# A software-pipelined attention and routing stage: a tile's sums move to the head of a step, its transposes a step later, and a group's ranks come from products with ones

## The chip, the cores and the metric

The kernel runs on 1 core of one Trainium2 chip. The metric is device time in microseconds (us) of one launch, lower is better. Engines are named as in the profile: PE is TensorE (PEld its weight loads), DVE is VectorE, ACT is ScalarE, POOL is GpSimd, SP is SyncE, which issues most of the DMAs.

## The reference

Three layers follow each other: a gated linear attention, a mixture of experts with one expert per token, and a gated linear unit with a norm. The change touches the first and the routing into the second.

```python
# attention: B, H, S, D = 4, 8, 768, 48
f = 1.0 / (1.0 + np.exp(-f_logit))
for t in range(S):
    state = f[:, :, t, :, None] * state + np.einsum('bhd,bhe->bhde', k[:, :, t], v[:, :, t])
    y[:, :, t] = np.einsum('bhd,bhde->bhe', q[:, :, t], state)
# experts: N, D, E, F = 3072, 384, 8, 1024
logits = x @ w_gate + modality_bias[modality_id]
e_idx = np.argmax(logits, axis=1)
probs = np.exp(logits - logits.max(-1, keepdims=True))
probs /= probs.sum(-1, keepdims=True) + 1e-09
gate_w = probs[np.arange(N), e_idx]
...
    h = np.maximum(x[mask] @ w1[e], 0.0)
    out[mask] = gate_w[mask, None] * (h @ w2[e])
# gated linear unit: d_ff = 1536
xn = x / rms * rms_g
out = (silu(xn @ w_gate) * (xn @ w_val)) @ w_out
```

## The kernel before

**Tiles.** The 3072 tokens are cut into 24 tiles of 128: tile t is chunk t // 4 of batch t % 4, so that the recurrence over chunks of one batch goes from tile t to tile t + 4. Within a chunk the recurrence is a product: running sums of the log gates (`cum`), their exponentials (`em`, `ep`) multiplied into k and q, a masked product (`am`), and a state per batch.

**Steps.** `attention_fast` is written out by hand: a loop over steps s, in which each engine gets its instructions in program order. A tile goes through these pieces, each in a step of its own:

- `p0(t)`: a clamp of the gate logits on DVE (L105), then exp, ln and a cast on ACT (L107, L108, L113), and the low half `ll` on POOL (L115).
- `p1(t)`: the running sums `cum` on PE (L124, L125, into the PSUM tile `pm`), their clamp `bc` on DVE (L129), `em` and `ep` on ACT (L133), `kp` on DVE (L134), `qp` on POOL (L135), and two small DMAs on SP that bring the chunk's decay to `dd` (L138).
- `p2(t)`: eight transposes on PE (L152), copied out by DVE (`kt`) and ACT (`qt`) (L154).
- `p3(t)`: `pa` on PE (L163), the mask product `am` on DVE (L166).
- `p4(t)`: the output `py` on PE (L178, L180), its copy `xt` on ACT (L182), the minimum of the decays `gm` on DVE (L185), the state's update on PE (`pu`, L190), DVE (L197, L199) and POOL (L201). The last chunk (tiles 20 to 23) has no update, the first (0 to 3) no product with the state.
- `mix(t)`: the gate's parts of the logits on PE (L423, into another part of the PSUM tile `pu`), copied by ACT (`ql`, L425); `logits(t)`: their sum on PE (L435, into another part of `pm`).
- Tiles are routed in groups of 4, 4, 2, 3, 3, 2, 2, 1, 1, 1 and 1. At a group's last tile `logits` adds the bias on DVE (`lg`, L438), `route` picks the expert in five DVE operations (L447 to L459) and an exp on ACT (L462), `share` makes the gate's weight (L471 to L474), `ranks` counts on PE (L483, L484, into `pm`) and copies the result (L486), and `place` turns counts into row numbers on DVE (L497 to L511).
- `send(1)`: four transposes `px` on PE (L523), a scaled copy `xo` on ACT (L526), and a scatter by POOL to the expert's rows in DRAM (L527). In the steps of `TWICE` two tiles are sent.

In a step of before, PE gets p4 of tile s-4, logits of s-5, ranks of s-6, p3 of s-3, p2 of s-2, mix of s-4, `cum` of s-1, and px. ACT gets xt, qt, ql, em, ep, the gates' exp, ln and cast of tile s+1, and xo.

**What rides along.** `first(s, x)` runs, at slots 0 to 3 of a step, pieces of the first expert's work that `early` has put on a list: the choice of the expert (`regs`), loads and splits of its weights (`load`, `halves`: L787, L789), gathers (L766), transposes of the gathered rows (`turn`: L805, L715, L716) and, in the last steps, its products (`up`, `down`: L828, L842). After the loop the remaining experts and the gated unit follow, with PE as the busiest engine.

**Order.** Tiles of a pool wait for their buffers' last readers; each engine waits at the head of its own queue. Of PSUM, `pm`, `pu`, `pk`, `pq` and `py` have one bank each and `pa` two.

Of the kernel before, what the change touches and what calls it, by code (L numbers as in the profile page):

```python
# [7 lines left out]
F32 = mybir.dt.float32  # L8
# [3 lines left out]
AF = mybir.ActivationFunctionType  # L12
# [24 lines left out]

TWICE = (15, 16, 23, 26)
LCLAMP = 40.0
# [23 lines left out]
def attention_fast(tc, io, cst, ps, gate, plan, first):  # L63
    nc = tc.nc
    q, k, v, f = io
    ident, tri, mask4, onesc = cst["ident"], cst["tri"], cst["mask4"], cst["onesc"]
    gm = cst["gm"]
    with ExitStack() as ctx:
        ld = ctx.enter_context(tc.tile_pool(name="a_ld", bufs=4))
        wk = ctx.enter_context(tc.tile_pool(name="a_wk", bufs=2))  # L70
        st = ctx.enter_context(tc.tile_pool(name="a_st", bufs=1))
        NB = 3
        qp = [st.tile([P, H, 64], F32, name=f"qp{i}") for i in range(2)]
        kp = [st.tile([P, H, 64], F32, name=f"kp{i}") for i in range(NB)]
        dd = [st.tile([P, HP], F32, name=f"dd{i}") for i in range(6)]
        sb = st.tile([P, B, HP, 2 * D], F32, name="state")
# [3 lines left out]
        def blank():  # L80
            for x in (kp[1], qp[1], kp[2]):
                nc.gpsimd.memset(x[:, :, D:64], 0.0)
            for i in range(6):
                nc.gpsimd.memset(dd[i], 1.0)
            nc.vector.memset(ps["y"], 0.0)
# [16 lines left out]

        def p0(t):
            d = T[t]
            nc.vector.tensor_scalar_max(d["f"], d["f"], -LCLAMP)  # L105
            e = wk.tile([P, H * D], F32, tag="e", name="e")
            nc.scalar.activation(e, d["f"].rearrange("p h d -> p (h d)"), AF.Exp, scale=-1.0)  # L107
            nc.scalar.activation(e, e, AF.Ln, bias=onesc)  # L108
            if t == 0:
                d["l"] = e  # L110
                return
            lh = wk.tile([P, H * D], F32R, tag="lh", name="lh")
            nc.scalar.copy(lh, e)  # L113
# [4 lines left out]
        def p1(t):  # L118
            d = T[t]
            cum = pm[:, 0:DM]  # L120
# [11 lines left out]
            for x, sign in both if t else both[::-1]:  # L132
                nc.scalar.activation(x, b4, AF.Exp, scale=sign)  # L133
            nc.vector.tensor_tensor(out=kp[t % NB][:, :, 0:D], in0=d["k"], in1=em, op=ALU.mult)  # L134
# [34 lines left out]
        def p4(t):  # L169
# [33 lines left out]
        with tc.manual_schedule():  # L203
            for t, names in ((0, "fq"), (1, "f"), (0, "k"), (1, "q"), (1, "k"), (2, "f"), (0, "v"), (1, "v"), (2, "v")):
                load(t, names)
            p0(0)
            setup = gate.setup()
            for s in range(NTILE + 7):
                if s == 1:
                    blank()  # L210
                if s == 3:
                    next(setup)
                    nc.gpsimd.memset(sb, 0.0)
                if s == 7:
# [31 lines left out]
            first(NTILE + 7, 0)  # L246


def decay_flag(tc, top, cst, pt):

    nc = tc.nc
    m1 = top.tile([P, 1], F32, name="fl_m1")
    nc.vector.tensor_reduce(out=m1, in_=cst["gm"], op=ALU.min, axis=AX.X)
    pt = pt()[0:1, 0:P]
# [63 lines left out]
def attention_again(tc, cst, gate, xd):  # L318
    nc = tc.nc
    list(gate.setup())  # L320
    with tc.tile_pool(name="s_x", bufs=9) as xp:
        for t in range(NTILE):
# [7 lines left out]
            gate.logits(t)  # L330
            gate.turns(gate.route(t))
            gate.share(t)
            gate.ranks(t)
# [4 lines left out]
def consts(tc, top, st):  # L338
# [5 lines left out]
    onesc = c["onesc"] = st.tile([P, 1], F32, name="onesc")  # L344
    gm = c["gm"] = top.tile([P, HP], F32, name="gm")
    nc.vector.memset(onesc, 1.0)
# [9 lines left out]
class Gate:  # L356
# [12 lines left out]
    def fill(self, st, w_gate, bias, mod):  # L369
# [39 lines left out]
        nc.vector.tensor_tensor(out=self.tril, in0=cst["tri"].bitcast(F32), in1=cst["ident"], op=ALU.subtract)  # L409
        nc.vector.memset(self.base, 0.0)  # L410
        yield

# [27 lines left out]
    def route(self, t):  # L440
# [18 lines left out]
        nc.vector.tensor_tensor(out=oh, in0=eq, in1=mw.unsqueeze(2).to_broadcast(sh), op=ALU.is_equal)  # L459
        yield  # L460
        self.ex = wk.tile(sh, F32, tag="ex", name="ex")
        nc.scalar.activation(self.ex, sf, AF.Exp)  # L462

    def share(self, t):
# [6 lines left out]
        nc.vector.reduce_sum(sm, self.ex, axis=AX.X)  # L471
        nc.vector.tensor_scalar_add(sm, sm, 1e-9)
        self.gt = wk.tile([P, n], F32, tag="gt", name="gt", bufs=4)
        nc.vector.reciprocal(self.gt, sm)  # L474

    def ranks(self, t):
        if not self.last_of(t):
            return
        n = GROUPS[GOF[t]]
        nc, wk, pm = self.nc, self.wk, self.cst["pm"]  # L480
        self.roh, self.rgt = self.oh, self.gt
        o2 = self.oh.rearrange("p b e -> p (b e)")
        nc.tensor.matmul(pm[:, DM + 32:DM + 32 + n * E], self.tril, o2, start=True, stop=True)  # L483
        nc.tensor.matmul(pm[:, DM + 64:DM + 64 + n * E], self.one16, o2, start=True, stop=True)  # L484
        self.rt = wk.tile([P, 2, n * E], F32, tag="rt", name="rt")
        nc.vector.tensor_copy(self.rt, pm[:, DM + 32:DM + 96].rearrange("p (a x) -> p a x", a=2)[:, :, 0:n * E])  # L486

    def place(self, t):
# [4 lines left out]
        sh = [P, n, E]  # L493
        oh, gt = self.roh, self.rgt
        rt = self.rt.rearrange("p a (b e) -> p a b e", e=E)
        for b in range(n):
            nc.vector.tensor_tensor(out=self.base[:, b + 1, :], in0=self.base[:, b, :], in1=rt[:, 1, b, :], op=ALU.add)  # L497
            yield
# [220 lines left out]
class Experts:  # L719
# [194 lines left out]
    def early(self, plan, ps, pm):  # L914
# [77 lines left out]

        f = FIRST + 7
        on(f, 2, regs)
# [23 lines left out]
        on(n + 7, 0, down, 2)  # L1018
        on(n + 7, 0, halves, 7)
        on(n + 7, 0, up, 5)  # L1020
        on(n + 7, 0, halves, 7)
        on(n + 7, 0, down, 3)
        on(n + 7, 0, up, 6)
        on(n + 7, 0, ahead)
        on(n + 7, 0, down, 4)
        on(n + 7, 0, up, 7)
        for m in (5, 6):
            on(n + 7, 0, down, m)
        on(n + 7, 0, second)
        on(n + 7, 0, down, 7)  # L1030
        on(n + 7, 0, last)
        on(n + 7, 0, next, made)
        self.begun = d
# [342 lines left out]
def attention_experts_glu(  # L1376
# [24 lines left out]
    def layers(again):  # L1401
        flag = None
        with ExitStack() as ctx:
            n = "b" if again else "a"
            top = ctx.enter_context(tc.tile_pool(name="top" + n, bufs=1))
            counts = top.tile([P, B + 1, E], F32, name="counts" + n)
            c2 = ctx.enter_context(ExitStack())
            with ExitStack() as c0:
                plan = Plan(tc, c0, c2.enter_context(tc.tile_pool(name="pt" + n, bufs=1, side="right")), counts[:, 0, :])
                with ExitStack() as c1:  # L1410
# [73 lines left out]
```

## Time before and how to read its profile

| | |
|---|---|
| median of 3 runs | 922.44 us (922.26 to 926.68) |
| profiled execution, its own time | 928.45 us |
| its span, first to last instruction | 926.9 us |
| PE busy in the span | 851.5 us (92%) |
| DVE, ACT, POOL busy | 513.4 (55%), 351.8 (38%), 201.3 us (22%) |
| mean granted clock of TensorE | 0.975 |

The profile is one execution on the chip; its times are us from the span's start. A row of the timeline has the start, the duration, the engine, the source line, the operation, the tile written and the tiles read, and how often; brackets give the idle time of that engine just before, and what ended it. Matmuls are pipelined, so the distance from one group's start to the next tells more than a group's own duration. A table by stretches gives busy us and instruction counts of PE, PEld, DVE, ACT and POOL, then the granted clock (1.00 is 2.4 GHz, 0.50 is 1.2 GHz), the mean busy share of the DMA engines, and GB/s.

### The profile page before, as it was taken

To read this page: it belongs to the slowest core of one execution; us is meant where nothing else is said; L and a number is where in the kernel's file an instruction comes from. 1 tells how busy PE (TensorE), PEld (TensorE's weight loads), DVE (VectorE), ACT (ScalarE), POOL (GpSimd) and SP (SyncE) were. 2 spreads that over 40 slices of the span, in tenths; PEclk is the share of its full clock that TensorE was granted. 3 is DMA by queue.
4 is the path that set the end of the run, shared out by engine and by line. 5 is a ranking of instruction groups with operands and counts; after the bars stand their busy time and mean duration, and the time that the engine had idled before them with its cause. 6 is when DMAs were issued, how large, how long until landed. Compare 5 with 4: busy or idle time off the path is not lost.

```text
span 926.9 us, 13938 instructions
## 1 busy us (share of the span) xinstructions
PE 851.5 (92%) x5218; PEld 717.1 (77%) x5218; DVE 513.4 (55%) x1059; ACT 351.8 (38%) x637; POOL 201.3 (22%) x245
## 2 busy tenths in 40 slices
PE   5789696779999999899899999999999999999993
PEld 4678575667787887678687788888888888888883
DVE  5777687767576665544699937235433622622220
ACT  6656546533444554333433422231231232122121
POOL 4355546422321231112131210010010000001001
PEclk9999998899999999999999999999999999999998
DMA  9776657111653653625222200000000000000001
GB/s 178 140 147 130 132 125 191 61 61 45 200 176 126 194 160 106 124 71 186 69 84 58 64 35 1 0 35 1 1 35 1 1 17 18 1 1 35 1 1 38
DMA packets 145312, 70.66 MB, mean 76 GB/s; under 512 B 113056, under 2 KB 140192, under 8 KB 145232
## 3 DMA queue, kind: packets, MB, share of 16 engines
q1 hardware_dynamic: 140336, 55.18, 24.1%
q0 software_dynamic: 4896, 14.47, 4.6%
q8 instruction: 44, 0.72, 0.3%
q14 instruction: 36, 0.29, 0.1%
HBM read 60.08 MB, written 9.52 MB: 75 GB/s over the span
## 4 chain that ended last, share of the span: by engine, by line
issue 32%; PE 11%; DVE 6%; POOL 2%; DMA 1%; ACT 1%; POOLq 0%; DVEq 0%; ACTq 0%; SPq 0%
PE po L1321 3%; PE pg L1300 3%; PE pv L1300 3%; POOL out_dram L1332 2%; DVE h L1312 1%; DVE q L1151 1%; DVE t L1149 1%; DVE t L1150 1%; PE pr L1235 0%; DVE sg L1309 0%; DVE t L1148 0%; DVE hl L716 0%; DVE h L1311 0%; DMA r<-in_moe_w_val_dram 0%; DMA out_dram<-o,cid 0%
## 5 line engine op out<-in xcount | busy, mean ns | idle before, releaser
L1307 DVE TENSOR_TENSOR h<-sg,pv 128x512 f32<-128x512 f32 x60 | 41.2, 687 | 192.2 <-PE pv L1300 192.2
L1332 POOL DMA_INDIRECT out_dram<-o,cid x24 | 23.2, 965 | 363.5 <-ACT o L1330 361.4
L1306 ACT ACTIVATE sg<-pg 128x512 f32<-128x512 f32 x60 | 35.9, 598 | 147.3 <-PE pg L1300 147.3
L715 ACT CAST hh<-h 128x512 fp32r<-128x512 f32 x70 | 43.3, 620 | 124.1 <-DVE h L1307 113.2
L1300 PE MATMUL pv<-xh,w1h 128*128 128x512 f32 x216 | 85.6, 396 | 2.1 <-DVE xh L1273 2.1
L1300 PE MATMUL pg<-xh,w0h 128*128 128x512 f32 x216 | 86.2, 399 | 0.0
L1300 PE MATMUL pg<-xl,w0h 128*128 128x512 f32 x216 | 85.3, 397 | 0.4 <-DVE xl L716 0.4
L1300 PE MATMUL pv<-xh,w1l 128*128 128x512 f32 x216 | 85.2, 394 | 0.4 <-POOL w1l L1154 0.4
L1300 PE MATMUL pg<-xh,w0l 128*128 128x512 f32 x216 | 85.5, 396 | 0.0
L1300 PE MATMUL pv<-xl,w1h 128*128 128x512 f32 x216 | 85.1, 395 | 0.0
L789 DVE TENSOR_TENSOR l<-r,h 128x768 fp32r<-128x768 f32 x48 | 49.4, 1035 | 33.3 <-ACT h L787 33.0
L716 DVE TENSOR_TENSOR hl<-h,hh 128x512 fp32r<-128x512 f32 x70 | 48.4, 693 | 33.3 <-ACT hh L715 33.3
L1321 PE MATMUL po<-w2h,hh 128*128 128x384 f32 x280 | 62.2, 340 | 2.8 <-ACT hh L715 2.6
L1321 PE MATMUL po<-w2l,hh 128*128 128x384 f32 x280 | 61.7, 338 | 0.0
L1321 PE MATMUL po<-w2h,hl 128*128 128x384 f32 x280 | 61.5, 338 | 0.0
L1321 PEld LDWEIGHTS po<-w2h,hh 128*128 128x128 f32 x280 | 50.7, 188 | 10.1 <-ACT hh L715 4.9
L828 PE MATMUL ph<-xh,h 128*128 128x512 f32 x135 | 54.0, 400 | 0.6 <-ACT xh L715 0.6
L828 PE MATMUL ph<-xh,l 128*128 128x512 f32 x135 | 53.8, 399 | 0.0
L828 PE MATMUL ph<-xl,h 128*128 128x512 f32 x135 | 53.4, 395 | 0.2 <-DVE xl L716 0.2
L787 ACT CAST h<-r 128x768 fp32r<-128x768 f32 x48 | 39.7, 834 | 29.1 <-PE py L842 12.1
L1321 PEld LDWEIGHTS po<-w2l,hh 128*128 128x128 f32 x280 | 50.1, 188 | 0.0
L1321 PEld LDWEIGHTS po<-w2h,hl 128*128 128x128 f32 x280 | 50.1, 188 | 0.0
(316 smaller groups left out, 1822.1 us busy)
## 6 DMA issues: line engine op xcount, KB each, us to landing
r<-in_moe_w_dram SPq DMA_DIRECT2D x48, 384.0 KB, 3.4
f<-in_f_logit_dram SPq DMA_DIRECT2D x24, 192.0 KB, 3.2
q<-in_q_dram SPq DMA_DIRECT2D x24, 192.0 KB, 3.9
k<-in_k_dram SPq DMA_DIRECT2D x24, 192.0 KB, 3.6
v<-in_v_dram SPq DMA_DIRECT2D x24, 192.0 KB, 3.9
r<-in_moe_w_gate_dram SPq DMA_DIRECT2D x12, 384.0 KB, 5.0
r<-in_moe_w_val_dram SPq DMA_DIRECT2D x12, 384.0 KB, 3.5
r<-in_moe_w_out_dram SPq DMA_DIRECT2D x12, 384.0 KB, 3.6
```

The source lines that it names most:

```text
L715: nc.scalar.copy(hi, src)
L716: nc.vector.tensor_tensor(out=lo, in0=src, in1=hi.bitcast(F32), op=ALU.subtract)
L787: self.nc.scalar.copy(h, r)
L789: self.nc.vector.tensor_tensor(out=l, in0=r, in1=h.bitcast(F32), op=ALU.subtract)
L828: nc.tensor.matmul(ph, a[:, kk, c], b[:, kk, 0:T], start=(n == 0), stop=(n == 8))
L1149: V.scalar_tensor_tensor(out=t, in0=top, scalar=-0x40000000, in1=t, op0=ALU.bitwise_and, op1=ALU.bitwise_or)
L1150: V.scalar_tensor_tensor(out=t, in0=low, scalar=29, in1=t, op0=ALU.logical_shift_right, op1=ALU.bitwise_or)
L1300: nc.tensor.matmul(p, a[:, kk, :], b[:, kk, :], start=(n == 0), stop=(n == 8))
L1306: nc.scalar.activation(sg, ps[0], AF.Silu)
L1307: nc.vector.tensor_tensor(out=h, in0=sg, in1=ps[1], op=ALU.mult)
L1321: self.nc.tensor.matmul(po[t], a[:, c], b[:, 0, :], start=(m == 0 and i == 0), stop=(m == self.KF - 1 and i == 2))
L1332: self.apart.add(nc.gpsimd.indirect_dma_start(out=self.out, out_offset=bass.IndirectOffsetOnAxis(ap=self.cid[:, i:i + 1], axis=0), in_=o, ...
```

## The change

From step 4 on, a step begins with p1 of tile s-1 (split into `p1e`, the sums and exponentials, and `p1p`, the products and DMAs), with the clamp of p0 (`p0f`) between them. Then come route of the group that ends at tile s-7, p4 of tile s-4, the exp of that group, the rest of p0 (`p0l`), logits of tile s-6 (before s-5), p3, mix of tile s-5 (before s-4), p2, share and ranks, place, and one send. The loop has 32 steps instead of 31, and the first expert's pieces move by one step with it. The order of the first four steps stays.

The minimum of the decays is not kept tile by tile: `dd` becomes one tile with a place for each of the 24, reduced once at the end. `kp` has four buffers instead of three. The constant 1e-9 is added by a `tensor_tensor` with a tile instead of a `tensor_scalar_add`. The ranks of a group come from n products on the shifted one-hots (its own tile with `tril`, earlier ones with `one16`) and n products for the sums, accumulated in PSUM, now in the bank of `pu`; `place` reads them there, so that the copy `rt`, the n running additions and the copy of the base fall away, and one addition keeps the base.

```diff
-TWICE = (15, 16, 23, 26)
+TWICE = (16, 17, 24, 27)
...
-        NB = 3
+        NB = 4
-        dd = [st.tile([P, HP], F32, name=f"dd{i}") for i in range(6)]
...
         def p0(t):
+            p0f(t)
+            p0l(t)
+        def p0f(t):
+            nc.vector.tensor_scalar_max(T[t]["f"], T[t]["f"], -LCLAMP)
+        def p0l(t):
             d = T[t]
-            nc.vector.tensor_scalar_max(d["f"], d["f"], -LCLAMP)
...
-            x = dd[t % 6]
             for h in range(2):
-                nc.sync.dma_start(x[64 * h:64 * h + D, :], ep[P - 1:P, h])
+                nc.sync.dma_start(dd[64 * h:64 * h + D, t, :], ep[P - 1:P, h])
...
-            x = dd[t % 6]
-            nc.vector.tensor_tensor(out=gm, in0=gm, in1=x, op=ALU.min)
+            x = dd[:, t]
...
-            for s in range(NTILE + 7):
+            for s in range(NTILE + 8):
...
                 first(s, 0)
+
+                full = s >= 4
+                ahead = 0 <= s - 1 < NTILE
+                if full and ahead:
+                    p1e(s - 1)
+                    if s + 1 < NTILE:
+                        p0f(s + 1)
+                    p1p(s - 1)
+                gate.turns(gate.route(s - 7))
                 if 0 <= s - 4 < NTILE:
                     p4(s - 4)
+                gate.exps(s - 7)
+                if full and s + 1 < NTILE:
+                    p0l(s + 1)
                 if s in TWICE:
                     gate.send(1)
-                gate.logits(s - 5)
-                gate.ranks(s - 6)
+                gate.logits(s - 6)
                 first(s, 1)
                 if 0 <= s - 3 < NTILE:
                     p3(s - 3)
+                gate.mix(s - 5)
                 if 0 <= s - 2 < NTILE:
                     p2(s - 2)
                 T.pop(s - 5, None)
-                gate.mix(s - 4)
+                gate.share(s - 7)
+                gate.ranks(s - 7)
                 first(s, 3)
-                gate.turns(gate.route(s - 5))
-                if 0 <= s - 1 < NTILE:
-                    p1(s - 1)
-                gate.turns(gate.place(s - 6))
-                if s + 1 < NTILE:
+                gate.turns(gate.place(s - 7))
+                if not full:
+                    if ahead:
+                        p1(s - 1)
                     p0(s + 1)
-                gate.share(s - 5)
                 gate.send(1)
                 first(s, 2)
...
-        nc.vector.tensor_scalar_add(sm, sm, 1e-9)
+        nc.vector.tensor_tensor(out=sm, in0=sm, in1=self.eps.to_broadcast([P, n]), op=ALU.add)
...
-        nc.tensor.matmul(pm[:, DM + 32:DM + 32 + n * E], self.tril, o2, start=True, stop=True)
-        nc.tensor.matmul(pm[:, DM + 64:DM + 64 + n * E], self.one16, o2, start=True, stop=True)
-        self.rt = wk.tile([P, 2, n * E], F32, tag="rt", name="rt")
-        nc.vector.tensor_copy(self.rt, pm[:, DM + 32:DM + 96].rearrange("p (a x) -> p a x", a=2)[:, :, 0:n * E])
+        rk, sums = pu[:, 192:192 + n * E], pu[:, 224:224 + E]
+        for j in range(n):
+            nc.tensor.matmul(rk[:, j * E:n * E], self.one16 if j else self.tril, o2[:, 0:(n - j) * E], start=(j == 0), stop=(j == n - 1))
+        for b in range(n):
+            nc.tensor.matmul(sums, self.one16, o2[:, b * E:(b + 1) * E], start=(b == 0), stop=(b == n - 1))
...
-        for b in range(n):
-            nc.vector.tensor_tensor(out=self.base[:, b + 1, :], in0=self.base[:, b, :], in1=rt[:, 1, b, :], op=ALU.add)
-            yield
-        nc.vector.tensor_tensor(out=ps_, in0=rt[:, 0], in1=self.base[:, 0:n, :], op=ALU.add)
+        nc.vector.tensor_tensor(out=ps_, in0=rk.rearrange("p (b e) -> p b e", e=E), in1=self.base.unsqueeze(1).to_broadcast(sh), op=ALU.add)
         yield
-        nc.vector.tensor_copy(self.base[:, 0, :], self.base[:, n, :])
+        nc.vector.tensor_tensor(out=self.base, in0=self.base, in1=sums, op=ALU.add)
...
-        f = FIRST + 7
+        f = FIRST + 8
...
-        on(n + 5, 0, up, 3)
-        on(n + 5, 0, down, 1)
-        on(n + 5, 2, next, made)
-        on(n + 7, 0, up, 4)
+        on(n + 6, 0, up, 3)
+        on(n + 6, 0, down, 1)
+        on(n + 6, 2, next, made)
+        on(n + 8, 0, up, 4)
```

## Rows read from the trace of the kernel before

**Rows 1.** Busy time in the stretch of the attention stage.

```profile
20.00:225.00 205.00, 166.90 (x2025) 140.52 (x2022) 148.60 (x421) 113.99 (x222) 95.88 (x126) 0.93 0.52 118
```

**Rows 2.** What PE waited for from 20 to 225 us: total, times, longest.

```profile
PE pu L423 <- ACT xt L182: 11.3, 7, 3.8
PE px L523 <- ACT xo L526: 8.3, 3, 3.9
...
PE pu L423 <- DVE state L197: 2.3, 1, 2.3
```

**Rows 3.** Timeline of the step that ends at 97 us: DVE, ACT, PE.

```profile
93.63 0.35 DVE L105 TENSOR_SCALAR f<-f 128x384 f32<-128x384 f32 x1
...
94.08 0.52 ACT L107 ACTIVATE e<-f 128x384 f32<-128x384 f32 x1 [2.90 <-DVE f L105]
...
96.17 0.58 ACT L182 COPY xt<-py 128x512 f32<-128x512 f32 x1
...
96.80 0.42 PE L423 MATMUL pu<-xt,wg 128*32 128x128 f32 x8 [3.17 <-DVE mx L447]
```

**Rows 4.** Timeline of PE in a step without a stall inside.

```profile
132.94 0.43 PE L423 MATMUL pu<-xt,wg 128*32 128x128 f32 x8 [0.40 <-ACT xt L182]
...
133.76 0.60 PE L523 MATMUL px<-ident,xt 128*128 128x128 f32 x4
134.29 0.43 PE L178 MATMUL py<-qt,state 128*48 128x128 f32 x4
...
138.03 0.66 PE L152 MATMUL pk<-ident,kp 128*128 128x128 f32 x4
138.53 0.60 PE L152 MATMUL pq<-ident,qp 128*128 128x128 f32 x4
```

**Rows 5.** Timeline of DVE over one step with `place` and into the next.

```profile
162.19 0.69 DVE L716 TENSOR_TENSOR xl<-pt,xh 128x512 fp32r<-128x512 f32 x1 [1.83 <-ACT xh L715]
162.79 0.55 DVE L129 TENSOR_SCALAR bc<-pm 128x384 f32<-128x384 f32 x1
163.93 0.56 DVE L134 TENSOR_TENSOR kp<-k,em 128x384 f32<-128x384 f32 x1 [0.59 <-ACT em L133]
164.41 1.59 DVE L497 TENSOR_TENSOR countsa<-countsa,rt 128x8 f32<-128x8 f32 x3
...
167.19 0.95 DVE L789 TENSOR_TENSOR l<-r,h 128x768 fp32r<-128x768 f32 x1
...
168.13 0.71 DVE L199 TENSOR_TENSOR state<-state,pu 48x192 f32<-48x192 f32 x2
...
168.96 1.28 DVE L166 TENSOR_TENSOR am<-pa,mask 128x512 f32<-128x512 f32 x2
...
173.79 0.16 DVE L447 TENSOR_REDUCE mx<-lg 128x2 f32<-128x16 f32 x1
...
174.60 0.17 DVE L459 TENSOR_TENSOR oh<-eq,mw 128x16 bf16<-128x16 f32 x1
```

**Rows 6.** Timeline of POOL at two of its products `qp`.

```profile
154.42 1.20 POOL L135 TENSOR_TENSOR qp<-q,ep 128x384 f32<-128x384 f32 x1 [2.63 <-ACT ep L133]
...
164.78 1.19 POOL L135 TENSOR_TENSOR qp<-q,ep 128x384 f32<-128x384 f32 x1 [3.82 <-ACT ep L133]
```

**Rows 7.** Timeline of DVE: the addition of 1e-9 at two places.

```profile
154.49 1.15 DVE L472 TENSOR_SCALAR sm<-sm 128x3 f32<-128x3 f32 x1
...
195.49 0.17 DVE L472 TENSOR_SCALAR sm<-sm 128x2 f32<-128x2 f32 x1
```

**Rows 8.** Timeline of DVE and PE: the state's update, and the next `mix`.

```profile
125.03 0.72 DVE L199 TENSOR_TENSOR state<-state,pu 48x192 f32<-48x192 f32 x2
...
125.90 0.43 PE L423 MATMUL pu<-xt,wg 128*32 128x128 f32 x8 [1.32 <-DVE state L199]
```

**Rows 9.** Timeline of PE: the second product of `ranks` in one group.

```profile
129.59 0.17 PE L484 MATMUL pm<-oh,one 128*128 128x24 bf16 x1
```

**Rows 10.** Busy time in the stretch behind PE's longest wait of the stage.

```profile
112.60:119.70 7.10, 7.00 (x44) 5.86 (x44) 2.11 (x4) 1.96 (x5) 3.79 (x6) 0.54 0.67 161
```

More of the change, by code (lines that the diff above doesn't have):

```diff
@@ L66, in attention_fast @@
     ident, tri, mask4, onesc = cst["ident"], cst["tri"], cst["mask4"], cst["onesc"]
-    gm = cst["gm"]
+    dd = cst["gm"]
     with ExitStack() as ctx:
@@ L80, in blank @@
         def blank():
-            for x in (kp[1], qp[1], kp[2]):
+            for x in (kp[1], qp[1], kp[2], kp[3]):
                 nc.gpsimd.memset(x[:, :, D:64], 0.0)
-            for i in range(6):
-                nc.gpsimd.memset(dd[i], 1.0)
             nc.vector.memset(ps["y"], 0.0)
@@ L118, in p1, with p1e @@
         def p1(t):
+            p1e(t)
+            p1p(t)
+        def p1e(t):
             d = T[t]
@@ L133, in p1, with p1p @@
                 nc.scalar.activation(x, b4, AF.Exp, scale=sign)
+            d["em"], d["ep"] = em, ep
+        def p1p(t):
+            d = T[t]
+            em, ep = d["em"], d["ep"]
             nc.vector.tensor_tensor(out=kp[t % NB][:, :, 0:D], in0=d["k"], in1=em, op=ALU.mult)
             nc.gpsimd.tensor_tensor(out=qp[t % 2].rearrange("p (a x) d -> p a x d", x=2)[:, :, :, 0:D], in0=d["q"].rearrange("p (a x) d -> p a x d", x=2), in1=ep.rearrange("p x d a -> p a x d"), op=ALU.mult)
-            x = dd[t % 6]
             for h in range(2):
-                nc.sync.dma_start(x[64 * h:64 * h + D, :], ep[P - 1:P, h])
+                nc.sync.dma_start(dd[64 * h:64 * h + D, t, :], ep[P - 1:P, h])
         def p2(t):
@@ L234, in attention_fast @@
                 T.pop(s - 5, None)
-                gate.mix(s - 4)
+                gate.share(s - 7)
+                gate.ranks(s - 7)
                 first(s, 3)
-                gate.turns(gate.route(s - 5))
-                if 0 <= s - 1 < NTILE:
-                    p1(s - 1)
-                gate.turns(gate.place(s - 6))
-                if s + 1 < NTILE:
+                gate.turns(gate.place(s - 7))
+                if not full:
+                    if ahead:
+                        p1(s - 1)
                     p0(s + 1)
-                gate.share(s - 5)
                 gate.send(1)
                 first(s, 2)
-            first(NTILE + 7, 0)
+            first(NTILE + 8, 0)
 def decay_flag(tc, top, cst, pt):
@@ L252, in decay_flag @@
     m1 = top.tile([P, 1], F32, name="fl_m1")
-    nc.vector.tensor_reduce(out=m1, in_=cst["gm"], op=ALU.min, axis=AX.X)
+    nc.vector.tensor_reduce(out=m1, in_=cst["gm"].rearrange("p t a -> p (t a)"), op=ALU.min, axis=AX.X)
     pt = pt()[0:1, 0:P]
@@ L331, in attention_again @@
             gate.turns(gate.route(t))
+            gate.exps(t)
             gate.share(t)
@@ L344, in consts @@
     onesc = c["onesc"] = st.tile([P, 1], F32, name="onesc")
-    gm = c["gm"] = top.tile([P, HP], F32, name="gm")
+    gm = c["gm"] = top.tile([P, NTILE, HP], F32, name="gm")
     nc.vector.memset(onesc, 1.0)
@@ L410, in fill @@
         nc.vector.memset(self.base, 0.0)
+        self.eps = st.tile([P, 1], F32, name="eps")
+        nc.vector.memset(self.eps, 1e-9)
         yield
@@ L459, in route, with exps @@
         nc.vector.tensor_tensor(out=oh, in0=eq, in1=mw.unsqueeze(2).to_broadcast(sh), op=ALU.is_equal)
-        yield
-        self.ex = wk.tile(sh, F32, tag="ex", name="ex")
-        nc.scalar.activation(self.ex, sf, AF.Exp)
+        self.sf = sf
+    def exps(self, t):
+        if not self.last_of(t):
+            return
+        self.ex = self.wk.tile(list(self.sf.shape), F32, tag="ex", name="ex")
+        self.nc.scalar.activation(self.ex, self.sf, AF.Exp)
     def share(self, t):
@@ L479, in ranks @@
         n = GROUPS[GOF[t]]
-        nc, wk, pm = self.nc, self.wk, self.cst["pm"]
-        self.roh, self.rgt = self.oh, self.gt
+        nc, pu = self.nc, self.ps["u"]
+        rk, sums = pu[:, 192:192 + n * E], pu[:, 224:224 + E]
         o2 = self.oh.rearrange("p b e -> p (b e)")
-        nc.tensor.matmul(pm[:, DM + 32:DM + 32 + n * E], self.tril, o2, start=True, stop=True)
-        nc.tensor.matmul(pm[:, DM + 64:DM + 64 + n * E], self.one16, o2, start=True, stop=True)
-        self.rt = wk.tile([P, 2, n * E], F32, tag="rt", name="rt")
-        nc.vector.tensor_copy(self.rt, pm[:, DM + 32:DM + 96].rearrange("p (a x) -> p a x", a=2)[:, :, 0:n * E])
+        for j in range(n):
+            nc.tensor.matmul(rk[:, j * E:n * E], self.one16 if j else self.tril, o2[:, 0:(n - j) * E], start=(j == 0), stop=(j == n - 1))
+        for b in range(n):
+            nc.tensor.matmul(sums, self.one16, o2[:, b * E:(b + 1) * E], start=(b == 0), stop=(b == n - 1))
+        self.rt = rk, sums
     def place(self, t):
@@ L493, in place @@
         sh = [P, n, E]
-        oh, gt = self.roh, self.rgt
-        rt = self.rt.rearrange("p a (b e) -> p a b e", e=E)
-        for b in range(n):
-            nc.vector.tensor_tensor(out=self.base[:, b + 1, :], in0=self.base[:, b, :], in1=rt[:, 1, b, :], op=ALU.add)
-            yield
+        oh, gt = self.oh, self.gt
+        rk, sums = self.rt
         ps_ = wk.tile(sh, F32, tag="ps", name="ps_")
-        nc.vector.tensor_tensor(out=ps_, in0=rt[:, 0], in1=self.base[:, 0:n, :], op=ALU.add)
+        nc.vector.tensor_tensor(out=ps_, in0=rk.rearrange("p (b e) -> p b e", e=E), in1=self.base.unsqueeze(1).to_broadcast(sh), op=ALU.add)
         yield
-        nc.vector.tensor_copy(self.base[:, 0, :], self.base[:, n, :])
+        nc.vector.tensor_tensor(out=self.base, in0=self.base, in1=sums, op=ALU.add)
+        yield
         nc.vector.tensor_tensor(out=ps_, in0=ps_, in1=self.cap[:, 0:n], op=ALU.add)
@@ L1013, in early @@
         on(n + 4, 0, down, 0)
-        on(n + 5, 0, up, 3)
-        on(n + 5, 0, down, 1)
-        on(n + 5, 2, next, made)
-        on(n + 7, 0, up, 4)
[L1018 to L1026, printed above, removed]
-        for m in (5, 6):
[L1028 to L1032, printed above, removed]
+        on(n + 6, 0, up, 3)
+        on(n + 6, 0, down, 1)
+        on(n + 6, 2, next, made)
+        on(n + 8, 0, up, 4)
+        on(n + 8, 0, down, 2)
+        on(n + 8, 0, halves, 7)
+        on(n + 8, 0, up, 5)
+        on(n + 8, 0, halves, 7)
+        on(n + 8, 0, down, 3)
+        on(n + 8, 0, up, 6)
+        on(n + 8, 0, ahead)
+        on(n + 8, 0, down, 4)
+        on(n + 8, 0, up, 7)
+        for m in (5, 6):
+            on(n + 8, 0, down, m)
+        on(n + 8, 0, second)
+        on(n + 8, 0, down, 7)
+        on(n + 8, 0, last)
+        on(n + 8, 0, next, made)
         self.begun = d
@@ L1405, in layers @@
             top = ctx.enter_context(tc.tile_pool(name="top" + n, bufs=1))
-            counts = top.tile([P, B + 1, E], F32, name="counts" + n)
+            counts = top.tile([P, E], F32, name="counts" + n)
             c2 = ctx.enter_context(ExitStack())
             with ExitStack() as c0:
-                plan = Plan(tc, c0, c2.enter_context(tc.tile_pool(name="pt" + n, bufs=1, side="right")), counts[:, 0, :])
+                plan = Plan(tc, c0, c2.enter_context(tc.tile_pool(name="pt" + n, bufs=1, side="right")), counts)
                 with ExitStack() as c1:
```

## The prediction

> **What bounds the kernel now.** The page's busy shares come first: PE has 92% of the span, so only a stretch in which it idles can give time back. All parts of the change lie in the attention stage, so I asked the sums of that stretch alone. From 20 to 225 us PE is busy 166.9 of 205 us, so 38.1 us are idle, and the granted clock is 0.93 in the mean [rows 1]: 14% of the stretch, 28.7 us, at 1.2 GHz. If PE was busy then, half of that, 14.4 us, is lost. Together 52.5 us is what a perfect order could give back; DVE, the next, is busy 148.6 us [rows 1].
>
> The waits come next. PE waited for xt 11.3 us in 7 places and for xo 8.3 us in 3 [rows 2]. One place shows why. DVE comes to the clamp L105 only at 93.63, behind `place`; ACT has stood 2.90 us for it, works through exp, ln, cast and xo, and only then copies xt at 96.17; PE's mix starts at 96.80 after 3.17 us without work [rows 3]. (The releaser named there, mx, ended at the same moment as xt.) The next `cum` is queued behind that mix, then bc, em, ep, and the next step's exp and xt: the step is a ring PE, DVE, ACT, PE, and any delay on DVE goes round it.
>
> A step without a stall shows the other limit. From mix at 132.94 to pq at 138.53, plus half a microsecond for pq itself (pk to pq is 0.50), PE needs 6.1 us [rows 4]. The stage has 24 tiles in 205 us with some tail, about 8.2 us each.
>
> **The change part by part.** *The order.* After it, mix takes an xt of the step before, logits a ql of the step before, and `cum` comes first. In a step without routing the dependences that stay inside are: cum, bc (0.55), em, kp, state, mix. From bc's start to kp's end is 164.49 - 162.79 = 1.70 us, and the state takes 0.71 [rows 5]; with three hand-offs of 0.1 mix could start 2.7 us after cum. In PE's queue py, pu, logits and pa lie between, 138.03 - 134.29 = 3.74 us [rows 4]. Slack 1.0: such a step is PE's 6.1 us. `am` (1.28) has mix, p2, px and cum to be ready in, over 2.5 us. ACT's xt waits for py, which ends about when ep does. I cost the move at nothing there; were that cover gone, each microsecond of lateness on DVE would be one on PE.
>
> The two DMAs of dd now leave SP early in the step; behind them stand the loads of the next step, needed two steps later. The loads get denser: the DMA engines are busy 0.52 at 8.2 us a step [rows 1], so 4.3 us per step, hidden under 6.1. The fourth kp buffer and the wide dd cost nothing in time; the buffers keep the earlier writes from waiting for the readers three steps on.
>
> *A step with routing.* Route's five operations, from mx at 173.79 to oh's end at 174.77 [rows 5], 1.0 us, now stand before the state: 2.7 + 1.0 = 3.7, just the slack. But qp starts on POOL about when ep ends, in the middle of route. Three additions of two SBUF tiles took 1.59 us from 164.41 while qp ran from 164.78 to 165.97 [rows 5, 6]; three like mx take about 0.6, so DVE stood about 1.0. So mix is between 0 and 1.2 late; I take 1.0, as eq and oh read two SBUF tiles and fall into qp's time. Six groups before the tail: 6.0 us.
>
> That mix waits for the state at all rests on the bank: they touch different columns of pu, yet mix starts at 125.90, behind a state that ends at 125.75 [rows 8]. The PSUM page of the Trainium skill (PSUM — Partial Sum Buffer, PSUM bank collisions raise a hardware error) wants PSUM guarded by bank and not by address; the trace agrees, by those 0.15 us. By that rule the ranks, now in pu, join this chain.
>
> *Ranks.* 48 products instead of 22, 26 more. A record shows 0.17 us [rows 9], overlap makes it less: between 0 and 4.4 us, I take 2.5. On DVE the copy rt, 13 additions, the copies of the base and 24 minima fall away. They are on no path of the new step except where DVE is late, so I count no gain.
>
> *The 1e-9.* With a `tensor_scalar` it took 1.15 us beside qp and 0.17 without [rows 6, 7]. The additions that stood beside qp [rows 5] show that a `tensor_tensor` of two SBUF tiles is held as well. What helps is its place, behind kt, where POOL is past qp. If it is held by another POOL product, up to 1.0 in a group's step, DVE is late for the next bc, which has 1.7 us until logits needs pm. Between 0 and 6, I take 0.
>
> The SBUF page (SBUF — State Buffer, SBUF: two separate sides) calls the pair of ports that DVE and GpSimd share an exclusive lock, also against DVE operations with two SBUF inputs; the trace agrees by the 1.59 us [rows 5]. By it this edit alone gives nothing.
>
> *What stays or is new.* The switch of orders at step 4: cum waits for the bc just before, 1.2 (cum about 0.5, bc 0.55, hand-offs). The setup of the gate in step 7: PE waited 2.3 us for the state behind it [rows 2]; it stays, 2.3. The choice of the first expert and a split L789 (0.95 [rows 5]) make DVE late twice by about half a microsecond: 1.0. The three steps with transposed rows: PE's transposes wait for kt's read of their bank, which comes about 2.0 us after pa (am 1.28, then kt of about 0.7), while PE has 1.35 of mix and p2 to do there, so 0.7; and DVE stands 1.83 us for xh and then has xl, 0.69 [rows 5], 2.5 in all, of which logits' wait for bc absorbs 1.7 to 2.0; so about 1.3 a step, 3.8. The tail: steps 28 and 29 leave PE 3.5 and 1.0 us of work (an estimate from the distances between PE's groups [rows 4] and the list of `early`), while a group's chain, lg, route, ranks, place, some 15 operations of 0.2, takes 3.5; step 30 has its products early enough. With smaller waits in 26 to 28: 4.5. Half clock after what gaps are left: 3.0, a fifth of today's. Hand-offs and denser DMA traffic: 3.0.
>
> Sum: 6.0 + 2.5 + 1.2 + 2.3 + 1.0 + 3.8 + 4.5 + 3.0 + 3.0 = 27.3. Gain 52.5 - 27.3 = 25.2 us. From 225 us on nothing changes but the start. The profiled execution took 928.45 us, so its like would take 903; the median of the runs shown is 6.0 lower, 922.44, and I take the gain off that: 897.
>
> **The rivals.** *Near PE's limit.* No hold by qp (0 for 6.0), ranks cheap (1), clock whole and no friction (0 for 3.0 and 3.0): returns of 13.8, 922.4 - 38.7 = 884. For it: DVE loses some 59 small operations, over 9 us at 0.16 each; against: the steps with turns.
>
> *DVE and the bank become the ring.* If the state comes 1.0 late in each of the 16 steps that update one after the first chunk, not only in the six counted (10 more), and the tail and turns cost double (8.3 more), the gain is 7: 915. For it: bc, kp and the state stand in one in-order queue with everything else; against: 1.0 us of slack in the plain step.
>
> *No change.* The ring is not what the stage waits for: another thing, the loads say, comes 25 us later anyway, and the time stays about 922. Against: the DMA engines are at 0.52 [rows 1].
>
> *Slower, by the clock.* After its 3.9 us wait for xo [rows 2], PE ran the next 7.1 us at 0.54 [rows 10], which cost some 3 us. If the new order, with a small gap in each step instead of a large one in some, held the lower clock over the work of six steps, 36.6 us would be lost to it where I count 3.0: 897 - 3.0 + 36.6 = 931. It decides from a loss of 28.2 us, a mean granted clock of the stage under about 0.86 (14% of 205 us). Against: the steps at 133 us ran whole behind a gap of 0.40 [rows 4].
>
> **How the numbers follow.** Forecast (890 to 905) 0.50; near the limit 0.18; the bank's ring 0.19; no change 0.06; slower 0.07. A difference under 0.5%, 4.6 us, can't be told from none. Faster 0.87, same 0.06, slower 0.07. The range leaves out slower, half of no change and a little at the lower end: 882 to 915.
>
> **What would show it.** In the profile after: PE's waits for xt and xo gone from the list; copies xt about 6.2 us apart in plain steps and 7 to 8 in routing steps; PE's idle time in the stage under 20 us; the last product of the stage near 200 us; clock 0.97 or more. Wrong it would be if mix waited for the state in plain steps, if ACT's em waited for bc by several microseconds, or if the clock stayed under 0.93.

## The result and the profile after

| | before | after |
|---|---|---|
| median | 922.35 us (921.16 to 926.68, 4 runs) | 893.8 us (891.53 to 895.43, 4 runs) |
| ratio of after to before | | 0.968, 95% interval 0.9643 to 0.9718 |
| profiled execution, its span | 928.45 us, 926.9 us | 891.53 us, 889.9 us |

The changed kernel is 28.6 us faster; 25.2 was forecast, 897 us. The stage ends with the last px. The first product of `up` behind it, before and after:

```profile
225.35 0.48 PE L828 MATMUL ph<-xh,h 128*128 128x512 f32 x1
```

```profile
194.66 0.48 PE L856 MATMUL ph<-xh,h 128*128 128x512 f32 x1
```

So the stretch that answers to [rows 1] now ends at 194.3 us (the columns as there):

```profile
20.00:194.30 174.30, 155.91 (x2057) 134.50 (x2057) 136.11 (x364) 112.60 (x222) 95.53 (x126) 0.96 0.63 139
```

PE is idle for 174.3 - 155.9 = 18.4 us (before: 38.1 [rows 1]), and a clock of 0.96 means 8% of the stretch at 1.2 GHz, a loss of 7.0 us if PE was busy then (before: 14.4). That is 27.1 us won in the stage: 19.7 from idle time, 7.4 from the clock. The stretch is 30.7 us shorter, 3.6 more: busy time less the clock's loss is 148.9 us, against 152.5 before. About 1.9 of these 3.6 can come from the rounding of the two clocks; the rest is not explained. The two profiled executions differ by 37.0 us in span and the medians by 28.6, since the execution of before lies 6 us above its median and that of after 2 us below.

What PE waits for in that stretch (total, times, longest) answers to [rows 2]:

```profile
PE pu L447 <- DVE state L209: 7.0, 5, 2.4
PE pu L447 <- DVE state L207: 2.8, 2, 2.4
PE pu L513 <- DVE oh L483: 2.6, 2, 2.5
PE pt L833 <- DVE kt L165: 2.5, 3, 1.5
PE pm L459 <- DVE bc L136: 1.8, 2, 1.2
PE pm L131 <- DVE bc L136: 1.6, 1, 1.6
PE pu L513 <- ACT ql L449: 1.3, 3, 0.4
```

The two entries that led the list before, xt with 11.3 us and xo with 8.3, are gone. First among those left is what the prediction put first: `mix` behind the state (L209; L207 is the same for the first chunk). The step of the first routed group, in the order of time:

```profile
57.63 1.20 POOL L147 TENSOR_TENSOR qp<-q,ep 128x384 f32<-128x384 f32 x1 [2.39 <-ACT ep L140]
57.77 1.12 DVE L477 SCALAR_TENSOR_TENSOR eq<-sf,w 128x32 f32<-128x32 f32 x1
...
59.25 0.71 DVE L209 TENSOR_TENSOR state<-state,pu 48x192 f32<-48x192 f32 x2
...
60.01 0.43 PE L447 MATMUL pu<-xt,wg 128*32 128x128 f32 x8 [0.76 <-DVE state L209]
...
61.30 0.18 PE L513 MATMUL pu<-oh,tril 128*128 128x32 bf16 x1
...
61.33 0.22 PE L513 MATMUL pu<-oh,one 128*128 128x24 bf16 x3
...
61.40 0.24 PE L515 MATMUL pu<-oh,one 128*128 128x8 bf16 x4
...
61.50 0.59 ACT L165 COPY qt<-pq 128x512 f32<-128x512 f32 x1 [0.73 <-PE pq L163]
61.51 0.63 PE L551 MATMUL px<-ident,xt 128*128 128x128 f32 x4
```

As foreseen, `eq` takes 1.12 us beside `qp` (0.18 elsewhere), the state is late, and PE loses 0.76 us. The eight products of `ranks` are over in 0.21 us, from 61.30 to the start of px at 61.51.

The longest of the five waits at L209 has another cause, in the step at 112 us. DVE and POOL, then PE's `mix`:

```profile
110.41 0.98 POOL L555 DMA_INDIRECT xe<-xo,pi  x1 [3.12 <-PE pu L447]
...
111.42 1.21 POOL L147 TENSOR_TENSOR qp<-q,ep 128x384 f32<-128x384 f32 x1
...
111.75 0.56 DVE L136 TENSOR_SCALAR bc<-pm 128x384 f32<-128x384 f32 x1
...
112.22 3.50 DVE L105 TENSOR_SCALAR f<-f 128x384 f32<-128x384 f32 x1
...
112.58 0.83 POOL L211 TENSOR_TENSOR state<-state,gm 128x384 f32<-128x384 f32 x1
...
113.36 1.00 POOL L118 TENSOR_TENSOR ll<-e,lh 128x384 fp32r<-128x384 f32 x1
...
114.32 1.18 POOL L147 TENSOR_TENSOR qp<-q,ep 128x384 f32<-128x384 f32 x1
...
115.65 0.55 DVE L146 TENSOR_TENSOR kp<-k,em 128x384 f32<-128x384 f32 x1
...
117.82 0.42 PE L447 MATMUL pu<-xt,wg 128*32 128x128 f32 x8 [2.42 <-DVE state L209]
```

The clamp, 0.35 us where POOL rests, stands for 3.50 us while POOL goes through four operations without a pause. POOL had stood 3.12 us ahead of a scatter, with the first of these operations queued behind it; what the scatter waited for the trace doesn't settle. The change moved the clamp from the end of a step to between `bc` and `kp`; it takes 13.7 us in 20 places from 20 to 205 us, 7.0 before. But the clamp is only what happened to stand there: in the run without it, below, `kp` is held as long.

### The profile page after: what moved, and what is told of

It is laid out like the page before. It is cut to its first block, busy times and chain, and to the rows that moved or that the text cites. A ratio compares the mean times of both kernels' runs of the same rounds, so it can differ in the third digit from the quotient of the medians.

```text
span 889.9 us, 13869 instructions
## 1 busy us (share of the span) xinstructions
PE 836.4 (94%) x5244; PEld 709.1 (80%) x5244; DVE 500.7 (56%) x1001; ACT 350.2 (39%) x637; POOL 200.5 (23%) x240
## 4 chain that ended last, share of the span: by engine, by line
issue 33%; PE 10%; DVE 7%; POOL 2%; DMA 1%; ACT 1%; SPq 0%; POOLq 0%; ACTq 0%
PE po L1349 4%; PE pv L1328 3%; PE pg L1328 3%; POOL out_dram L1360 2%; DVE q L1179 1%; DVE t L1177 1%; DVE t L1178 1%; DVE h L1340 1%; DVE sg L1337 1%; DVE hl L744 0%; DVE t L1176 0%; DMA r<-in_moe_w_out_dram 0%; DVE h L1339 0%; DVE rr L1288 0%; DMA out_dram<-o,cid 0%
## 5 line engine op out<-in xcount | busy, mean ns | idle before, releaser
L1328 PEld LDWEIGHTS pv<-xh,w1h 128*128 128x128 f32 x216 | 40.6, 188 | 11.9 <-DVE xh L1301 2.3
```

What stands on the lines that cost most here:

```text
L1328: nc.tensor.matmul(p, a[:, kk, :], b[:, kk, :], start=(n == 0), stop=(n == 8))
```

## The experiments

Each ratio is to the kernel before, run on the same chip; after the change it is 0.968. I took the theory of the ring (DVE late, ACT's exp, xo and xt, PE's `mix`, and round again) against the rival that the work DVE is relieved of carries the gain.

**Order alone.** The changed kernel with the old bookkeeping:

```diff
+            nc.vector.tensor_tensor(out=cst["least"], in0=cst["least"], in1=x, op=ALU.min)
...
-        nc.vector.tensor_tensor(out=sm, in0=sm, in1=self.eps.to_broadcast([P, n]), op=ALU.add)
+        nc.vector.tensor_scalar_add(sm, sm, 1e-9)
...
-        self.rt = rk, sums
+        nc.tensor.matmul(pm[:, DM + 32:DM + 32 + n * E], self.tril, o2, start=True, stop=True)
+        nc.tensor.matmul(pm[:, DM + 64:DM + 64 + n * E], self.one16, o2, start=True, stop=True)
+        self.rt = wk.tile([P, 2, n * E], F32, tag="rt", name="rt")
```

> The new order of the steps, with the old bookkeeping: two products for ranks, copied from pm to rt, an addition for each tile of a group, the minimum gm for every tile, the tensor_scalar for the 1e-9. Theory (the ring DVE, ACT, PE set the stage, and the order alone breaks it): 24 us under the kernel before, about 898, within 5 us of the changed kernel. Rival (what DVE no longer has to do carries the gain): less than half of it, about -12, 910. Both theories leave xt and xo out of PE's waits.

Measured: 898.9 us, ratio 0.9743 (0.9681 to 0.9804). The order alone gives some 24 of the 28.6 us (18 to 29 by the interval), and neither xt nor xo is left among PE's waits for `mix` and px.

**Bookkeeping alone.** The kernel before, its loop and its three `kp` buffers untouched, with that diff the other way round:

```diff
-            nc.vector.tensor_tensor(out=gm, in0=gm, in1=x, op=ALU.min)
...
-        nc.vector.tensor_scalar_add(sm, sm, 1e-9)
+        nc.vector.tensor_tensor(out=sm, in0=sm, in1=self.eps.to_broadcast([P, n]), op=ALU.add)
...
+        self.rt = rk, sums
```

> The old order of the steps, with the new bookkeeping: ranks and counts from products with ones in pu, no copy rt, no minima for each tile, the 1e-9 as a tensor_tensor. Theory (the ring stays, and only DVE's share of the delays in steps with routing shrinks): -9 us, between -5 and -14, about 913, and PE still waits for xt and xo some 15 us. Rival (the relief of DVE carries the gain): -20, about 902, and these waits are mostly gone. A third case, that these operations were on no path: within 2 us of the kernel before.

Measured: 925.1 us, ratio 1.0027 (0.9997 to 1.0056): nothing won, so both named outcomes with a gain fail. The third, on no path, fits the time, but PE's waits show another reason. From 20 to 205 us PE waited:

```profile
PE pu L483 <- DVE state L194: 10.7, 4, 3.0
PE px L521 <- ACT xo L524: 8.5, 3, 3.4
PE pu L420 <- ACT xt L178: 7.6, 5, 2.2
```

The ring's two waits stand, and a new one leads: `ranks` (L483) now write the state's bank, right behind products whose reader on DVE is late. Moved behind `mix`:

```diff
-                gate.ranks(s - 6)
...
                 gate.mix(s - 4)
+                gate.ranks(s - 6)
```

> The old order with the new bookkeeping, as in the run of that name, but the products for ranks behind mix and the transposes, not between logits and pa. There PE had waited 10.7 us in 4 places for the state, since ranks now write the state's bank. Theory (that wait ate what the relief of DVE gave): 5 to 12 us under the kernel before, about 914, ratio 0.991. Rival (the relief is on no path of the old order): within 2 us of the kernel before, xt and xo waited for as in it.

Measured: 918.4 us, ratio 0.9949 (0.9928 to 0.997). The wait for the state is gone, xt (10.5 us) and xo (7.7) stay. So the bank's wait had eaten what the relief gives, and that is some 4 to 5 us, a little under the 5 to 12 expected. The order alone and the whole change lie 5.8 us apart, of the same size, though their intervals overlap.

In the kernel of bookkeeping alone the addition of 1e-9, now a `tensor_tensor`, took 979 ns in the mean; the `tensor_scalar` of before took 898 in the same stretch. With the new order it is 277 and 273. The form of the instruction changes little, its place does.

**Which part of the order.** First mix, logits and the gate's parts one step earlier again, `cum` still first:

```diff
-                gate.mix(s - 5)
+                gate.mix(s - 4)
```

> The changed kernel with mix, logits and the gate's parts one step earlier again: sums come first in the step, but mix takes the xt copied in the same step, logits a ql of the step before. Theory (what counts is that cum, bc, em and kp come ahead in the queues; xt is ready 2.8 us after cum, mix comes at 3.7): within 3 us of the changed kernel, perhaps 3 faster for one step less in the tail. Rival (the greater age of mix's xt is what breaks the ring): PE waits for xt again, and the time is 10 us or more above the changed kernel.

Measured: 895.75 us, ratio 0.9699 (0.9637 to 0.9761), no difference from the changed kernel that can be told. `mix` does wait for xt again, as the rival has it, but for 1.3 us in four places, 0.4 the longest. Then the reverse, sums last and `mix` later (from the changed kernel):

```diff
-                full = s >= 4
-                ahead = 0 <= s - 1 < NTILE
-                if full and ahead:
-                    p1e(s - 1)
...
+                gate.ranks(s - 7)
...
                 gate.mix(s - 5)
...
+                gate.turns(gate.route(s - 6))
+                gate.exps(s - 6)
+                if 0 <= s - 1 < NTILE:
+                    p1(s - 1)
```

> The changed kernel with the sums back at the end of the step and only mix, logits and the gate's parts one step later; ranks and counts from products with ones as in the changed kernel. Theory (either edit of the order alone breaks the ring): 22 us under the kernel before, about 900. Rival (the place of the sums is what counts): PE's waits move from xt to bc or the state, and no more than 12 us are gained, 910 or above.

Measured: 923.85 us, ratio 1.0009 (0.9982 to 1.0036). My theory falls. But `ranks` again waited 9.6 us for the state in 4 places, so I ran it with them behind `mix`:

```diff
-                gate.ranks(s - 7)
...
                 gate.mix(s - 5)
+                gate.ranks(s - 7)
```

> The old place of the sums, mix, logits and the gate's parts one step later, and the ranks behind mix, where they don't wait for the state: the run of ranks late (918), with the age of mix's xt as the only addition. Theory (a product that takes its xt a step later doesn't cut the ring, since exp still stands for the clamp behind place, and ACT's xo and PE's px behind them): xt gone from PE's waits, px's wait for xo of 8 us stays, 3 us or less gained, about 916, ratio 0.993. Rival (mix's wait was what closed the ring, and only the bank's wait hid it in the earlier run): 905 or less.

Measured: 916.1 us, ratio 0.9928 (0.9903 to 0.9952). PE's waits from 20 to 205 us:

```profile
PE px L543 <- ACT xo L546: 10.7, 9, 3.9
PE pu L505 <- ACT ql L440: 5.1, 9, 1.1
...
PE py L189 <- ACT xt L193: 0.6, 1, 0.6
```

`mix` is not on the list for xt any more, and the ring closes through xo and px: ACT has exp ahead of xo, and exp waits for DVE's clamp (16.5 us in 9 places). A later `mix` cuts one of two ways round and gains 2 us, with intervals that overlap. So the link to cut is exp's place. The next run moves only the clamp with exp, ln, the cast and `ll` behind it, in the old order with ranks late:

```diff
+                if 0 < s < NTILE:
+                    p0f(s)
                 if 0 <= s - 4 < NTILE:
                     p4(s - 4)
+                if 0 < s < NTILE:
+                    p0l(s)
...
-                if s + 1 < NTILE:
-                    p0(s + 1)
```

> The kernel of ranks late (918: old order, new bookkeeping, ranks behind mix), with one move: the clamp, exp, ln, cast and ll of a tile are issued not at the end of a step but behind py and the state of the next, so that xt and the xo before it no longer stand behind exp on ACT. The sums stay last in the step, and mix takes the xt of its own step. Theory (the ring of the prediction goes through exp, which waits for DVE's late clamp ahead of xo and xt, and cutting that one link is what the new order does): xt and xo gone from PE's waits, 905 or less, ratio under 0.98. Rival (what counts is that cum, bc and kp come ahead of the rest of the step): the wait moves to another product, 914 or above, ratio over 0.99.

Measured: 902.6 us, ratio 0.9777 (0.9751 to 0.9802): 16 us under the kernel with ranks late, as the theory had it. Its waits:

```profile
PE pu L491 <- ACT ql L430: 9.1, 9, 1.7
PE px L529 <- ACT xo L532: 2.7, 2, 1.3
...
PE pu L428 <- DVE state L200: 2.1, 4, 1.1
```

xt is down from 10.5 to 0.4 us and xo from 7.7 to 2.7, while exp itself waits for the clamp as long as it did (10.8 us in 8 places, 11.2 in 7 with ranks late): what counts is what stands behind it. What is left to the changed kernel, some 9 us, is of the size of the wait of `ranks` for ql, whose bank they write; so how much the sums' place adds beyond exp's stays open.

**What is left: route.** The whole of `route` behind `py` and the state:

```diff
-                gate.turns(gate.route(s - 7))
                 if 0 <= s - 4 < NTILE:
                     p4(s - 4)
+                gate.turns(gate.route(s - 7))
```

> The changed kernel with the gate's route moved from before py and the state to behind them. Theory (mix waits for the state because route's five operations and the hold by qp stand before it on DVE): PE's wait for the state at L209 falls from 7.0 us to under 4, and the time by 3 to 5 us, to about 890, ratio 0.964 to the kernel before. Rival (the state is late for other reasons, the clamp f held beside POOL above all): the wait stays near 7 us and the time within 2 us of the changed kernel's 894.

Measured: 902.45 us, ratio 0.9778 (0.9759 to 0.9797), some 9 us slower than the change. The wait for the state did fall, from 7.0 to 3.0 us, but see the first routed group:

```profile
59.90 0.83 POOL L211 TENSOR_TENSOR state<-state,gm 128x384 f32<-128x384 f32 x1
59.97 0.80 DVE L474 TENSOR_TENSOR sf<-lg,mx 128x32 f32<-128x32 f32 x1
...
60.30 0.43 PE L447 MATMUL pu<-xt,wg 128*32 128x128 f32 x8
...
60.80 0.23 ACT L490 ACTIVATE ex<-sf 128x32 f32<-128x32 f32 x1 [1.67 <-DVE sf L474]
...
62.55 0.26 ACT L449 COPY ql<-pu 128x128 f32<-128x128 f32 x1
...
62.86 0.18 PE L513 MATMUL pu<-oh,tril 128*128 128x32 bf16 x1 [1.11 <-DVE am L177]
```

`mix` runs without a wait, `sf` is held beside POOL instead, and ACT stands for it 1.67 us with exp, ln, the cast and ql queued behind. `ranks` start when ql's copy is over (am, the releaser named, had begun at 61.55 and takes 1.29): their waits for ql rise from 1.3 to 5.2 us. The wait has moved to the engine that feeds the ring. That is not the whole of the 9 us: the products of `up` behind the last px begin 6.4 us later than in the changed kernel (201.08 against 194.66), and the rest lies behind the stage or in the spread. Another 1.4 us, `py` behind ACT's ln before any group is routed, has no cause in this edit. With only `eq`, `mw` and `oh` behind the state:

```diff
-                gate.turns(gate.route(s - 7))
+                gate.turns(gate.peak(s - 7))
                 if 0 <= s - 4 < NTILE:
                     p4(s - 4)
+                gate.turns(gate.route(s - 7))
```

> The changed kernel with route in two: the row maximum mx and sf stay ahead of the state, so that ACT gets ex in time; eq, mw and oh come behind the state. In the run with the whole of route behind the state, sf was held 0.80 us beside POOL, ACT stood for it ahead of exp, ln and the cast, ql came late and ranks, which write its bank, waited for it. Theory (that was the price, and three of route's five operations before the state are what mix waits for): mix's wait for the state under 4 us, ranks' wait for ql back under 2, and 2 to 4 us faster than the changed kernel, about 891, ratio 0.965. Rival (whatever stands behind the state delays am, kt and with them something else): 895 or above.

Measured: 893.5 us, ratio 0.9682 (0.9655 to 0.9709). Waits for the state at L209 fall to 4.4 us, not quite under 4, of which 2.3 are again the step behind the late scatter; those for ql are back at 1.3, as expected. Those for kt and bc rise by 0.5 and 0.9, and the time is that of the change, between the theory's 891 and the rival's 895: the rival's reason, without a loss that can be told.

**What is left: the clamp.** Back to the end of a step, for the tile after next:

```diff
-                    if s + 1 < NTILE:
+                    if s == 4:
                         p0f(s + 1)
...
+                elif s + 2 < NTILE:
+                    p0f(s + 2)
```

> The changed kernel with the clamp f of a tile one step earlier, at the end of a step behind place, where it stood before the change; exp, ln and the cast stay where the change put them. Theory (between bc and kp the clamp falls beside POOL's operations and waits for f's load, 13.7 us in 20 steps where 7.0 would do, and this makes the state late): clamp back to 0.35 us each, the wait of 2.4 us for the state near 118 us and the one behind the DMA at 32 us gone, 4 to 5 us faster, about 889, ratio 0.964. Rival (it is held at the new place as well, by the next tile's ll, or the cover of 1 us takes it up): within 2 us of the changed kernel.

Measured: 902.55 us, ratio 0.9779 (0.9759 to 0.9798), slower by some 9 us. The clamp takes 13.4 us, no less than where the change put it. DVE's wait for `em` from 20 to 205 us, and ACT's wait for `bc`, show what was lost:

```profile
DVE kp L146 <- ACT em L140: 11.9, 20, 0.7
```

```profile
ACT em L140 <- DVE bc L136: 29.2, 20, 4.3
```

They were 6.6 (17 places) and 18.1 us. Between `bc` and `kp` DVE waits for `em` anyway and the clamp fills that time; at the end of a step it stands in front of `bc`, and PE's wait for `bc` in `logits` rises from 1.8 to 5.5 us. Both moves, the diffs of the clamp and of the whole route, together:

> Both moves: route behind the state, and the clamp at the end of the step before. Theory (two separate causes of one wait): the waits for the state under 2 us in all, 7 us faster than the changed kernel, about 887, ratio 0.961. Rival (one cause seen twice): no more than the better of the two alone, 889 to 894.

Measured: 904.2 us, ratio 0.9801 (0.978 to 0.9822): no better than either, the theory falls with its parts. And the clamp left out:

```diff
-            nc.vector.tensor_scalar_max(T[t]["f"], T[t]["f"], -LCLAMP)
+            pass
```

> The changed kernel without the clamp of f at -40, which is left out of the computation. Theory (between bc and kp the clamp fills the time in which DVE waits for em, so only what it is held beside POOL and its wait for f's load cost anything, 13.7 - 7.0 + 2.1 = 8.8 us of DVE, part of it under the 1 us of slack): 3 to 6 us faster than the changed kernel, about 890, ratio 0.964; kp's wait for em grows by about 7 us. Rival (the holds are covered too): within 2 us of 894.

Measured: 891.1 us, ratio 0.966 (0.9634 to 0.9686). `kp` waits for `em` 14.6 us, 8.0 more, as expected, and the waits behind the late load are gone (2.8 to 0.6 us), but those for the state at L209 are 7.8, no less than with the clamp. The longest is in the same step:

```profile
108.31 0.99 POOL L555 DMA_INDIRECT xe<-xo,pi  x1 [4.13 <-PE pq L163]
...
109.82 4.03 DVE L146 TENSOR_TENSOR kp<-k,em 128x384 f32<-128x384 f32 x1 [0.59 <-ACT em L140]
...
115.48 0.43 PE L447 MATMUL pu<-xt,wg 128*32 128x128 f32 x8 [3.16 <-DVE state L209]
```

`kp`, 0.56 us elsewhere, is now held through the same POOL operations, and in the two steps with splits for 1.00 and 1.57 us. So the hold is not the clamp's: it falls on the operation of DVE that meets POOL's run behind a late scatter, and leaving out the clamp doesn't take it away. The median is 2.7 us lower, between the theory and the rival, and the intervals overlap; what the holds cost stays open.

No version here beats the changed kernel by a difference that can be told from none.

## Why the prediction was right, step by step

**The ring** is shown: exp behind xt alone gives 16 us. One part of its telling was wrong. I let it close through xt and `mix` and had xo as a second sign; it closes through either, and an older xt for `mix` is worth nothing that can be told, by itself (0.9949 to 0.9928) or on top (0.9699 to 0.968).

**The returns.** 27.3 us were to be left of 52.5; 18.4 + 7.0 = 25.4 are. Term by term, from the timeline of the changed kernel (the hand-offs' 3.0 can't be told apart):

| term | predicted | found |
|---|---|---|
| mix behind the state, six groups | 6.0 | 7.0 in five places, two of them (0.76, 0.78) by route alone, 2.42 behind DVE held beside POOL |
| expert choice and splits | 1.0 | 1.07 and 1.97 of those 7.0, after splits held to 2.23 and 2.75 us and clamps to 1.47 and 1.48 |
| products of ranks | 2.5 | 0.7, an estimate: 0.21 for eight, so 0.026 for each of the 26 more |
| switch of orders | 1.2 | 1.57 |
| setup of the gate | 2.3 | 1.23 and 0.32 |
| turns | 3.8 | 0.34, 0.58 and 1.54 |
| tail | 4.5 | 2.45 (oh) and three times 0.44 (ql) |
| half clock | 3.0 | 7.0 |
| not counted: clamp behind its load | 0 | 2.45 |

The last row is a step that I overlooked. The clamp stands early now, and in step 5 its f is not there yet:

```profile
29.86 0.82 DVE L105 TENSOR_SCALAR f<-f 128x384 f32<-128x384 f32 x1 [2.06 <-DMA f<-in_f_logit_dram]
...
31.86 0.43 PE L447 MATMUL pu<-xt,wg 128*32 128x128 f32 x8 [2.45 <-DVE state L207]
```

Mis-sized were the clock (7.0 for 3.0) and the ranks (0.7 for 2.5). "No gain" for the relief of DVE was too low by 4 to 5 us in the old order; in the new one the 5.8 us are within the noise. The two terms that make `mix` wait came out at their size (7.0 for 6.0 and 1.0 together), but the reason foreseen, `eq` held by one `qp` in each of six groups, was seen in two places with 1.5 us together; the largest wait was DVE held through several POOL operations behind a late scatter, for which the sum had no term. These errors went both ways, so that the sum came so near was in part luck.

**The signs.** xt and xo gone and idle time under 20 us (18.4) hold; the stage ends at about 194.5 us, where 200 was said. Copies of xt are 5.3 to 5.9 us apart in plain steps, less than the 6.1 that PE seemed to need, and 7.2 to 7.7 in most routed ones. The clock is 0.96, not 0.97. Of the signs of being wrong, `mix` waited for the state in one plain step, step 5, behind the late load; `em` waited for `bc` 18.1 us in 20 places, 2.4 us the longest.

**The rivals.** Near PE's limit (884) wanted a whole clock and no hold; neither came. The ring of DVE and the bank (915) was real where I had not looked for it: in the old order `ranks` in the state's bank cost the whole relief. No change and slower by the clock are excluded; the mean clock rose.

## What to carry to other kernels

When engines with in-order queues wait for each other in a ring, look for the one instruction that waits for the late engine and has copies queued behind it that others need, and issue it behind them; moving the readers of these copies later leaves the second way round. A wait that is removed by reordering mostly reappears at the next product that shares the bank or the next operation on the freed engine, so price a move by what it is put in front of, not by its own length. An instruction is free only in a place where its engine waits anyway. And when an operation stands beside another engine's work, leave it out once before you blame it: here the hold went on to the next one.

## What the runs showed of the hardware

- A DVE operation from SBUF to SBUF can be held through several POOL operations that begin after it: 3.50 us through three such, behind a `qp` already running, for 0.35 us of work, and 4.03 us for the 0.56 us of `kp` in the run without the clamp. The Trainium skill (SBUF — State Buffer, SBUF: two separate sides) says that the engine that starts first gets the shared pair for the whole instruction and the other blocks; the trace agrees on the block, but the clamp had been waiting since 112.22 and was passed by operations that began at 112.58, 113.36 and 114.32.
- Small products cost almost nothing one after the other: eight in 0.21 us, 0.026 each, where a single record shows 0.17 to 0.18 [rows 9].
- Products into another part of a PSUM bank waited for that bank's reader on another engine: the state (10.7 us in 4 places, bookkeeping alone) and ql (9.1 us in 9, exp behind xt). The traces show the wait, not whether the chip or the program's semaphores impose it.
